# Rows of w, u and g turned by TensorE, an early activation table, and later DMA transposes in a fused linear-attention and MLP kernel

## The chip, the cores and the metric

The kernel runs on one core of a Trainium2 chip. The time is device microseconds (us) of one execution, taken as the median of several. Runs that lie over 1.5% above the fastest of the same kernel are called slow and left out of ratios. Five engines work side by side: TensorE (matmuls, "PE" in the profile, with its weight loads as "PEld"), VectorE (DVE), ScalarE (ACT), GpSimd (POOL) and SyncE (SP), which here mostly issues transfers for the DMA engines.

## The reference, cut to what matters

A linear-attention recurrence with a decay `w` per head and channel and a bonus `u` for the present token, then layer normalization and a two-layer MLP with a residual. There are 4 sequences of 768 tokens, 8 heads of 48 channels (384 in all) and 1536 hidden units.

```python
def _attn_ref(r, k, v, w, u):                      # (4, 8, 768, 48)
    state = np.zeros((B, H, D, D))
    for t in range(S):
        cur = np.einsum('bhd,bhe->bhde', u[None] * kt, vt)
        y[:, :, t] = np.einsum('bhd,bhde->bhe', rt, state + cur)
        state = w[None, :, :, None] * state + np.einsum('bhd,bhe->bhde', kt, vt)

def _moe_ref(x, g_ln, w_ch1, w_ch2):               # x: (4, 768, 384)
    xn = (x - mu) / np.sqrt(var + 1e-06) * g_ln
    return x + np.maximum(xn @ w_ch1, 0.0) @ w_ch2
```

## The kernel before

The tokens are cut into 24 tiles of 128, six to a sequence. In each tile, k and r are scaled by powers of w (tables `Fk` and `Fr`), which turns the recurrence inside a tile into matmuls: scores `at` = k·r, masked to `A`; the bonus from `q` = k·r elementwise; the state `Z`; and `y` from `A`, the state and v. The result is normalized (`xn`) and turned (`xT`) for the MLP: "up" matmuls into `hp`, ReLU into `hT`, "down" matmuls into `o`, and the store.

The scores and up matmuls of this kernel read k and xn with channels on the partitions, so both are transposed. Early tiles do it on TensorE, with a copy out of PSUM by ScalarE or VectorE. Later tiles let a DMA do it, with no instruction on TensorE. The constants `KP` and `LNP` are the first tile that uses DMA for k and for xn.

```python
    def transposes_k(i):                      # tiles below KP: TensorE, then evacuate_k
        for q in range(HP):
            nc.tensor.transpose(out=tk_t[i][:, q, :], in_=sc[:, q, :], identity=ident[:])
    def transpose_k_by_dma(i):                # tiles from KP on
        kT_t[i] = trp.tile([P, HP, P], BF16, name="kT", bufs=NKT)
        nc.sync.dma_start_transpose(out=kT_t[i][:], in_=k_bufs[i % NSC].rearrange("p h d -> p (h d)"))
    ...                                       # ln_by_dma(i) does the same for xn, from tile LNP on
    group_len = [1] * 2 + [GT] + [1] * 2 + [GT] * ((NT - 6) // GT)
    LNP = 4
    KP = 8
```

The order of all instructions is made by a list scheduler when the kernel is built. It places one task after another on a planned clock, always the one that can start first. A task has an engine, a cost, needs and buffers. A transfer also has a share of the DMA engines' time (`load`) and an extra delay until it has landed (`lands`).

```python
                key = (pick[1] - (...), -pri)          # pick[1]: planned start; ties go to the higher pri
    ...
            if t["load"]:
                dma_at = max(dma_at, end) + t["load"]
                end = dma_at + t["lands"]
    ...
            add(f"kT{i}", "SP", 1.25, lambda i=i: transpose_k_by_dma(i), [f"sck{i}"], ..., load=0.67, lands=1.2)
            add(f"lc{i}", "SP", 1.2, lambda i=i: ln_by_dma(i), [f"xn{i}", f"xT{g}"], ..., load=0.5, lands=1.2)
```

Each engine is given its own list in that order. Where something in it is late, the traces show the engine idle: TensorE for 10.7 us in front of DMA transposes in the kernel before. TensorE's MLP matmuls are strewn between the steps of the recurrence to fill its time; what is left of them runs after the last tile. Until the MLP starts, TensorE also runs dummy matmuls on an identity (`o<-ident`, "warming"): 177 of them, busy for 14.5 us, in the kernel before.

At the start, w is read element by element into a column, and u, w and g in the same way by ScalarE's queue:

```python
    w_c = const.tile([P, CK], FP32, name="w_c")
    nc.sync.dma_start(out=w_c[:], in_=bass.AP(tensor=w.tensor, offset=w.offset, ap=[[1, P], [P, CK]]))
    ...
    for src, dst in ((w, w_p), (u, u_p)):
        for par in range(2):
            nc.scalar.dma_start(out=dst[par * DP : par * DP + D, :],
                in_=bass.AP(tensor=src.tensor, offset=src.offset + par * D, ap=[[1, D], [E2, HP]]))
    load(0, "v", nc.scalar)
    g_sb = const.tile([P, CK], FP32, name="g_sb")
    nc.scalar.dma_start(out=g_sb[:], in_=moe_g_ln.rearrange("(kc p) -> p kc", p=P))
```

In the profile these small loads take long for their size: the 1.5 KB of `w_c` land after 2.7 us and those of `g_sb` after 5.4, where the median load of v by SyncE, 192 KB, takes 4.2.

## Time and profile before

The time before is 171.41 us (171.04 to 171.57, three runs). The profiled execution spans 168.1 us from the first instruction to the last.

| before | us | share of the span |
|---|---|---|
| TensorE busy | 148.4 | 88% |
| VectorE busy | 108.9 | 65% |
| ScalarE busy | 96.8 | 58% |
| GpSimd busy | 88.2 | 52% |
| TensorE waiting for a DMA transpose | 10.7 | 6% |

The busiest engine is TensorE, so the question is what it does in the 19.7 us in which it is idle. The prediction below shows those lines of the profile and reads them. One mark of progress is used throughout: the start of a tile's last recurrence matmul, "y of tile n". In the kernel before, y of tile 4 starts at 34.22 us and y of tile 23, the last, at 128.81.

### The profile page before, as it was taken

The page shows a single profiled execution, that of the slowest core. Times are in us where ns is not written, and L with a number is a line of the kernel's source. Part 1 is how long each engine was busy: PE and PEld are TensorE (multiplying, and loading weights), DVE is VectorE, ACT ScalarE, POOL GpSimd, SP SyncE. Part 2 cuts the span into 40 slices and gives each one's busy share as a digit, 9 for nine tenths or more (in the row PEclk, how much of TensorE's full clock was granted, in tenths as well). Part 3 has the DMA queues.
Part 4 walks back from the last instruction along what each step waited for, and adds up shares of the span by engine and source line. Part 5 has one row for each costly group of instructions (what it writes and reads, how often), then busy time and mean ns, then how long its engine had stood idle before and what let it go on. Part 6 is the DMA issues. An engine that isn't in the chain of part 4 may idle for free.

```text
span 168.1 us, 4543 instructions
## 1 busy us (share of the span) xinstructions
PE 148.4 (88%) x1774; PEld 114.6 (68%) x1774; DVE 108.9 (65%) x226; ACT 96.8 (58%) x217; POOL 88.2 (52%) x133
## 2 busy tenths in 40 slices
PE   6988998999594999979399999879999999999991
PEld 6887887687473677656257776657867777777660
DVE  5689979977982799787667887578985111111141
ACT  0665787698582468655715686547776654553200
POOL 2299849667665489665544669947985100000000
PEclk9999999999998799999959999999999999999999
DMA  3998999989989999899997999989913131111122
GB/s 71 212 232 217 397 201 340 304 196 216 201 191 157 184 169 231 193 161 199 150 192 182 183 185 252 185 154 204 193 31 98 47 94 51 47 47 47 51 94 94
DMA packets 87316, 27.95 MB, mean 166 GB/s; under 512 B 81536, under 2 KB 86144, under 8 KB 87296
## 3 DMA queue, kind: packets, MB, share of 16 engines
q1 hardware_dynamic: 75552, 24.13, 70.5%
q10 hardware_dynamic: 11744, 3.54, 10.9%
q8 instruction: 14, 0.23, 0.6%
q14 instruction: 6, 0.05, 0.1%
HBM read 18.88 MB, written 4.72 MB: 140 GB/s over the span
## 4 chain that ended last, share of the span: by engine, by line
PE 49%; DMA 22%; POOL 9%; SPq 5%; DVE 4%; issue 4%; ACT 4%; POOLq 0%; DVEq 0%; ACTq 0%
PE hp L577 18%; PE o L603 16%; DMA kT<-sc 13%; DMA xT<-xn 6%; PE o L285 3%; DMA v<-in_v_dram 3%; SPq L188 3%; PE at L401 3%; POOL Vb L437 3%; SPq L182 3%; PE hp L603 2%; POOL rs L530 1%; POOL sc L351 1%; PE tr L381 1%; POOL w_sb L332 1%
## 5 line engine op out<-in xcount | busy, mean ns | idle before, releaser
L577 PE MATMUL hp<-xT,w_sb 128*128 128x256 bf16 (+1 forms) x504 | 59.2, 261 | 4.2 <-DMA xT<-xn 4.2
L588 ACT ACTIVATE hT<-hp 128x512 bf16<-128x512 f32 x72 | 42.5, 597 | 29.9 <-PE hp L577 28.9
L603 PE MATMUL o<-w_sb,hT 128*128 128x384 bf16 x264 | 54.2, 332 | 0.6 <-DVE ot L613 0.3
L577 PEld LDWEIGHTS <-w_sb 128*128 128x128 bf16 x504 | 42.8, 99 | 13.3 <-issue 3.6
L603 PEld LDWEIGHTS <-hT 128*128 128x128 bf16 x288 | 27.2, 99 | 13.7 <-issue 1.8
L613 DVE SCALAR_TENSOR_TENSOR ot<-o,rs,x 128x384 f32<-128x384 f32 x22 | 13.5, 615 | 28.9 <-PE o L603 28.6
L412 DVE TENSOR_TENSOR A<-at,mask 128x512 bf16<-128x512 f32 x48 | 30.9, 681 | 1.0 <-PE at L401 1.0
L437 POOL TENSOR_TENSOR Vb<-v,cc 128x384 f32<-128x384 f32 x24 | 20.4, 850 | 9.3 <-ACT cc L433 9.2
L351 POOL TENSOR_TENSOR sc<-r,Fr 128x384 bf16<-128x384 f32 x15 | 15.9, 1063 | 13.1 <-DMA r<-in_r_dram 5.9
L501 DVE SCALAR_TENSOR_TENSOR x<-y,Vb 128x384 f32<-128x384 f32 x24 | 13.2, 548 | 7.5 <-PE y L488 5.7
L514 ACT ACTIVATE xn<-x,sum 128x384 bf16<-128x384 f32 x24 | 14.7, 613 | 5.5 <-DVE x L501 5.3
L348 POOL TENSOR_TENSOR sc<-k,Fk 128x384 bf16<-128x384 f32 x15 | 16.0, 1064 | 1.8 <-DMA k<-in_k_dram 1.0
L394 DVE TENSOR_TENSOR q<-rT,kT 128x512 bf16<-128x512 bf16 x20 | 13.0, 648 | 5.2 <-DMA kT<-sc 4.9
L401 PE MATMUL at<-rT,kT 48*128 48x128 bf16 x192 | 10.0, 226 | 6.7 <-DMA kT<-sc 6.5
L285 PE MATMUL o<-ident 128*128 128x128 bf16 x177 | 14.5, 239 | 1.6 <-DVE ident L240 1.6
L387 ACT COPY rT<-tr 128x512 bf16<-128x512 bf16 x17 | 11.9, 739 | 5.3 <-PE tr L381 3.6
L530 POOL TENSOR_TENSOR rs<-rs,expo 128x1 f32<-128x1 f32 x24 | 13.5, 564 | 2.0
L521 ACT ACTIVATE sq<-x,sum 128x384 bf16<-128x384 f32 x24 | 14.5, 604 | 0.0
L464 DVE TENSOR_TENSOR Z<-s,WLZ 128x384 bf16<-128x384 f32 x20 | 11.0, 550 | 4.1 <-ACT cc L433 3.6
L285 PEld LDWEIGHTS <-ident 128*128 128x128 bf16 x177 | 12.3, 109 | 1.8 <-DVE ident L240 1.6
L401 PEld LDWEIGHTS <-kT 48*128 48x128 bf16 x192 | 5.6, 97 | 10.9 <-DMA kT<-sc 8.6
L433 ACT COPY cc<-s 128x8 f32<-128x8 f32 x24 | 4.0, 167 | 11.4 <-PE s L453 9.0
(72 smaller groups left out, 168.5 us busy)
## 6 DMA issues: line engine op xcount, KB each, us to landing
wst<-in_moe_w_ch_dram SPq DMA_DIRECT2D x6, 768.0 KB, 6.7
r<-in_r_dram SPq DMA_DIRECT2D x11, 384.0 KB, 5.1
k<-in_k_dram SPq DMA_DIRECT2D x22, 192.0 KB, 4.8
v<-in_v_dram SPq DMA_DIRECT2D x18, 192.0 KB, 4.2
out_dram<-ot SPq DMA_DIRECT2D x16, 192.0 KB, 2.4
out_dram<-ot ACTq DMA_DIRECT2D x8, 192.0 KB, 1.9
v<-in_v_dram ACTq DMA_DIRECT2D x6, 192.0 KB, 4.5
k<-in_k_dram ACTq DMA_DIRECT2D x2, 192.0 KB, 4.1
```

The lines of the kernel that those rows point to most:

```text
L285: nc.tensor.matmul(out=warm[:, :P], lhsT=ident[:], rhs=ident[:], start=True, stop=True)
L348: eng.tensor_tensor(out=k_bufs[i % NSC][:, :, :D], in0=k_t[i][:], in1=Fk[:], op=ALU.mult)
L351: eng.tensor_tensor(out=r_bufs[e % NSR][:, j, :, :D], in0=r_t[e][:, :, j * D : (j + 1) * D], in1=Fr[:, j], op=ALU.mult)
L401: nc.tensor.matmul(out=at_t[i][:, par, p, :], lhsT=kT_t[i][p0 : p0 + D, p, :], rhs=rT_t[i][p0 : p0 + D, p, :], start=True, stop=True,)
L412: nc.vector.tensor_tensor(out=A_t[i][:, par], in0=at_t[i][:, par], in1=mask[:].unsqueeze(1).to_broadcast([P, HP, P]), op=ALU.mult,)
L437: nc.gpsimd.tensor_tensor(out=Vb_t[i][:], in0=vf_t[i][:], in1=cc_t[i][:].unsqueeze(2).to_broadcast([P, H, D]), op=ALU.mult)
L514: nc.scalar.activation(out=xn_t[i][:], in_=x_t[i][:], func=ACT.Identity, bias=sum_t[i][:], scale=-float(C))
L521: nc.scalar.activation(out=sq[:], in_=x_t[i][:], func=ACT.Square, bias=sum_t[i][:], scale=-float(C), accum_out=sq_t[i][:])
L530: nc.gpsimd.tensor_tensor(out=rs_t[i][:], in0=rs_t[i][:], in1=expo[:], op=ALU.pow)
L577: nc.tensor.matmul(out=hp[:, f * gw : (f + 1) * gw], lhsT=w1_sb[:, n, kc, fb * P : (fb + 1) * P], rhs=xT_t[g][:, kc, :gw], start=(kc == 0) ...
L588: nc.scalar.activation(out=hT_t[g][:, nf * m : nf * (m + 1), :gw], in_=hp_t[g, m][:].rearrange("p (f t) -> p f t", f=nf), func=ACT.Relu,)
L603: nc.tensor.matmul(out=o_t[i][:, :C], lhsT=hT_t[g][:, fk, j * P : (j + 1) * P], rhs=w2_sb[:, fk, :], start=(fk == 0), stop=(fk == FK - 1),)
```

## The change

It has two parts. The **start** loads w, u and g as rows, turns them with TensorE, and has ScalarE make a small copy first, meant to bring its activation table load forward (it starts at 4.13 us in the profile before and at 0.72 after; late_table below takes the copy out again). The **plan** moves DMA transposes to later tiles (k from tile 14 instead of 8, xn from tile 8 instead of 4), plans each with 3.0 instead of 1.2 us of landing time, makes the first six MLP groups single tiles, and asks for w1 two loads earlier.

```diff
-                dma_at = max(dma_at, end) + t["load"]
+                dma_at = max(dma_at, end + 1.2) + t["load"]
...
-    w_c = const.tile([P, CK], FP32, name="w_c")
-    nc.sync.dma_start(out=w_c[:], in_=bass.AP(tensor=w.tensor, offset=w.offset, ap=[[1, P], [P, CK]]))
+    w_row = const.tile([CK, P], FP32, name="w_row")
+    nc.sync.dma_start(out=w_row[:], in_=w.rearrange("h d -> (h d)").rearrange("(kc p) -> kc p", p=P))
...
-            nc.scalar.dma_start(                 # four column loads of w and u, one of g: gone
+    first = const.tile([P, 1], FP32, name="first")
+    nc.scalar.copy(out=first[:], in_=expo[:])
     load(0, "v", nc.scalar)
...
+    nc.gpsimd.dma_start(out=rows[0:CK, :], in_=moe_g_ln.rearrange("(kc p) -> kc p", p=P))
+    for n, src in enumerate((w, u)):
+        nc.gpsimd.dma_start(out=rows[CK + n * HP : CK + (n + 1) * HP, :]...[:, :, :D], in_=src...)
...
+    nc.tensor.transpose(out=wps[:, :CK], in_=w_row[:], identity=ident_f[:CK, :CK])
+    w_c = const.tile([P, CK], FP32, name="w_c")
+    nc.vector.tensor_copy(out=w_c[:], in_=wps[:, :CK])
...
-    group_len = [1] * 2 + [GT] + [1] * 2 + [GT] * ((NT - 6) // GT)
+    group_len = [1] * 6 + [GT] * ((NT - 6) // GT)
-    LNP = 4
-    KP = 8
+    LNP = 8
+    KP = 14
...
-    N1, N2 = 10, 13
+    N1, N2 = 8, 13
...
-                load=0.67, lands=1.2)            # k by DMA
+                load=0.67, lands=3.0)
-            add(f"lc{i}", ... load=0.5, lands=1.2)    # xn by DMA
+            add(f"lc{i}", ... load=0.5, lands=3.0)
```

Cut here: smaller constants of the plan, the turning of the rows of g, w and u into `vec` in the middle of the first tile, and `Fk` copied by ScalarE.

More of the change, by code (lines that the diff above doesn't have):

```diff
@@ L30, in add @@
     def add(self, name, eng, cost, fn, needs=(), takes=(), gives=(), pri=0, load=0.0, kind=None,
-            alt=None, lands=2.4):
+            alt=None, lands=1.9):
         t = dict(name=name, eng=eng, cost=cost, fn=fn, needs=list(needs), takes=list(takes),
@@ L53, in order @@
         eng_at = {e: 0.0 for e in self.LAG}
-        eng_at["SP"], dma_at = 4.0, 5.0
+        eng_at["SP"], dma_at = 3.5, 5.9
         last_kind = None
@@ L188, in load @@
         eng.dma_start(out=dst[:], in_=src[b, :, s0 : s0 + L, :].rearrange("h t d -> t h d"))
-    w_c = const.tile([P, CK], FP32, name="w_c")
-    nc.sync.dma_start(out=w_c[:], in_=bass.AP(tensor=w.tensor, offset=w.offset, ap=[[1, P], [P, CK]]))
+    w_row = const.tile([CK, P], FP32, name="w_row")
+    nc.sync.dma_start(out=w_row[:], in_=w.rearrange("h d -> (h d)").rearrange("(kc p) -> kc p", p=P))
     load(0, "r", nc.sync)
     load(0, "k", nc.sync)
-    w_p = const.tile([P, HP], FP32, name="w_p")
-    u_p = const.tile([P, HP], FP32, name="u_p")
-    nc.vector.memset(w_p[:], 0.0)
-    nc.vector.memset(u_p[:], 0.0)
-    for src, dst in ((w, w_p), (u, u_p)):
-        for par in range(2):
-            nc.scalar.dma_start(
-                out=dst[par * DP : par * DP + D, :],
-                in_=bass.AP(tensor=src.tensor, offset=src.offset + par * D, ap=[[1, D], [E2, HP]]),
-            )
+    NR = CK + 2 * HP
+    rows = const.tile([NR, P], FP32, name="rows")
+    nc.vector.memset(rows[:], 0.0)
+    expo = const.tile([P, 1], FP32, name="expo")
+    nc.vector.memset(expo[:], -0.5)
+    first = const.tile([P, 1], FP32, name="first")
+    nc.scalar.copy(out=first[:], in_=expo[:])
     load(0, "v", nc.scalar)
-    g_sb = const.tile([P, CK], FP32, name="g_sb")
-    nc.scalar.dma_start(out=g_sb[:], in_=moe_g_ln.rearrange("(kc p) -> p kc", p=P))
     NW = 3
@@ L240 @@
     nc.vector.tensor_copy(ident[:], ident_f[:])
-    expo = const.tile([P, 1], FP32, name="expo")
-    nc.vector.memset(expo[:], -0.5)
+    nc.gpsimd.dma_start(out=rows[0:CK, :], in_=moe_g_ln.rearrange("(kc p) -> kc p", p=P))
+    for n, src in enumerate((w, u)):
+        nc.gpsimd.dma_start(
+            out=rows[CK + n * HP : CK + (n + 1) * HP, :].rearrange("q (e d) -> q e d", e=2)[:, :, :D],
+            in_=src.rearrange("(q e) d -> q e d", e=2),
+        )
     expl = const.tile([P, 1], FP32, name="expl")
@@ L254, with keep_warm @@
     nc.vector.memset(uwI[:], 0.0)
+    warm = ps.tile([P, 512], FP32, name="o")
+    def keep_warm(n):
+        for _ in range(n):
+            nc.tensor.matmul(out=warm[:, :P], lhsT=ident[:], rhs=ident[:], start=True, stop=True)
     T = const.tile([P, CK, 2 * L], FP32, name="T")
@@ L272, in powers @@
         )
+    keep_warm(12)
+    wps = ps.tile([P, 512], FP32, name="s")
+    nc.tensor.transpose(out=wps[:, :CK], in_=w_row[:], identity=ident_f[:CK, :CK])
+    w_c = const.tile([P, CK], FP32, name="w_c")
+    nc.vector.tensor_copy(out=w_c[:], in_=wps[:, :CK])
     for kc in range(CK):
@@ L279 @@
         powers(T2[:, kc], w_r, kc)
-    warm = ps.tile([P, 512], FP32, name="o")
-    def keep_warm(n):
-        for _ in range(n):
-            nc.tensor.matmul(out=warm[:, :P], lhsT=ident[:], rhs=ident[:], start=True, stop=True)
-    keep_warm(38)
+    keep_warm(10)
     Fr = const.tile([P, 2, H, D], FP32, name="Fr")
@@ L297, with turn_rows, copy_rows, bonus_weights @@
         src = fps[:, :C].rearrange("p (h d) -> p h d", h=H)
-        if j < 2:
-            nc.scalar.copy(out=Fr[:, j], in_=src)
-        else:
-            nc.vector.tensor_copy(out=Fk[:], in_=src)
+        nc.scalar.copy(out=Fr[:, j] if j < 2 else Fk[:], in_=src)
+    vec = const.tile([P, NR], FP32, name="vec")
+    vps = ps.tile([P, 512], FP32, name="s")
+    w_p, u_p = vec[:, CK : CK + HP], vec[:, CK + HP : NR]
     g_neg = const.tile([P, CK], FP32, name="g_neg")
     wl = const.tile([P, HP], FP32, name="wl")
+    def turn_rows():
+        nc.tensor.transpose(out=vps[:, :NR], in_=rows[:], identity=ident_f[:NR, :NR])
+    def copy_rows():
+        nc.vector.tensor_copy(out=vec[:], in_=vps[:, :NR])
     def negate_g():
-        nc.vector.tensor_scalar(out=g_neg[:], in0=g_sb[:], scalar1=-1.0 / C, scalar2=None, op0=ALU.mult)
-    def bonus_weights():
+        nc.vector.tensor_scalar(out=g_neg[:], in0=vec[:, :CK], scalar1=-1.0 / C, scalar2=None, op0=ALU.mult)
+    def bonus_weights(eng):
         for par in range(2):
             p0 = par * DP
-            nc.gpsimd.tensor_tensor(
+            eng.tensor_tensor(
                 out=uwI[p0 : p0 + D, :, par], in0=u_p[p0 : p0 + D, :], in1=w_p[p0 : p0 + D, :], op=ALU.mult
@@ L316, in chunk_decay @@
     def chunk_decay():
-        nc.gpsimd.tensor_tensor(out=wl[:], in0=w_p[:], in1=expl[:].to_broadcast([P, HP]), op=ALU.pow)
+        nc.gpsimd.tensor_tensor(out=wl[:], in0=w_p, in1=expl[:].to_broadcast([P, HP]), op=ALU.pow)
     def spread_decay():
@@ L632 @@
     NU = {g: FK * n * P // 512 for g, n in enumerate(group_len)}
-    add("Fr", "ACT", 6.5, None, pri=99)
-    add("Fk", "DVE", 6.8, None, pri=99)
-    for name, lands in (("r0", 5.2), ("k0", 6.3), ("v0", 7.3), ("g", 8.5)):
+    add("scan", "DVE", 5.65, None, pri=99)
+    add("Fr", "ACT", 5.9, None, pri=99)
+    add("Fk", "ACT", 0.65, None, needs=["Fr"], pri=99)
+    for name, lands in (("r0", 5.4), ("k0", 6.4), ("v0", 7.5), ("rows", 5.5)):
         add(name, "", lands, None, pri=99, takes={"r0": [("r", 0, 2)], "k0": [("k", 0, 1)], "v0": [("vf", 0, 2)]}.get(name, []))
-    add("uw", "POOL", 0.45, bonus_weights, needs=["scr00"], pri=70)
-    add("wl", "POOL", 1.05, chunk_decay, needs=["uw"], pri=70)
+    add("turn", "PE", 0.15, turn_rows, needs=["rows", "Fk", "TR0", "TK0"], pri=70, takes=[("s", "vec", 1)])
+    add("vec", "DVE", 0.15, copy_rows, needs=["turn"], pri=70, gives=[("s", "vec")])
+    add("uw", "DVE", 0.3, bonus_weights, needs=["scr00", "vec"], pri=70, alt=[("POOL", 0.5)])
+    add("wl", "POOL", 1.1, chunk_decay, needs=["uw"], pri=70)
     add("WLZ", "ACT", 0.7, spread_decay, needs=["wl", "rT0", "kT0"], pri=70)
-    add("gn", "DVE", 0.2, negate_g, needs=["g", "A01"], pri=70)
+    add("gn", "DVE", 0.2, negate_g, needs=["vec", "A01"], pri=70)
     seq = [(a, i) for e in range(NT // 2) for a, i in (("r", 2 * e), ("k", 2 * e), ("v", 2 * e), ("k", 2 * e + 1), ("v", 2 * e + 1))]
-    N1, N2 = 10, 13
+    N1, N2 = 8, 13
     seq[N2:N2] = [("w2l", n) for n in range(NW)]
@@ L655 @@
         elif i and a == "r":
-            add(f"r{i // 2}", "SP", 0.6, lambda e, i=i: load(i, "r", e), takes=[("r", i // 2, 2)], pri=pri, load=1.58,
+            add(f"r{i // 2}", "SP", 0.6, lambda e, i=i: load(i, "r", e), takes=[("r", i // 2, 2)], pri=pri, load=1.5,
                 alt=[("ACT", 0.5)])
@@ L659 @@
             add(f"{a}{i}", "SP", 0.6, lambda e, i=i, a=a: load(i, a, e),
-                takes=[("k", i, 1)] if a == "k" else [("vf", i, 2)], pri=pri, load=1.05, alt=[("ACT", 0.5)])
+                takes=[("k", i, 1)] if a == "k" else [("vf", i, 2)], pri=pri, load=1.03, alt=[("ACT", 0.5)])
     for n in range(NW):
@@ L675 @@
         add(f"sckb{i}", "", 0.0, None, [], [("sck", i, 1 if last else 2)], pri=p0)
-        add(f"sck{i}", "DVE", 0.7, lambda e, i=i: scale_k(i, e), [f"k{i}", "Fk", f"sckb{i}"] + (["scr01"] if i == 0 else []), [], [("k", i)], pri=p0,
+        add(f"sck{i}", "DVE", 0.7, lambda e, i=i: scale_k(i, e), [f"k{i}", "Fk", f"sckb{i}"], [], [("k", i)], pri=p0,
             alt=[("POOL", 1.0)])
@@ L684 @@
                 [("scr", e)], pri=p0)
-        add(f"rT{i}", "ACT", 0.74, lambda g, i=i: evacuate_r(i, g), [f"TR{e}"], [("rT", i, 1)], [("tr", ("r", e))], pri=p0,
+        add(f"rT{i}", "ACT", 0.74, lambda g, i=i: evacuate_r(i, g), [f"TR{e}"] + (["kT0"] if i == 1 else []), [("rT", i, 1)], [("tr", ("r", e))], pri=p0,
             alt=[("DVE", 0.74)])
@@ L728 @@
         else:
-            add(f"lc{i}", "SP", 1.2, lambda i=i: ln_by_dma(i), [f"xn{i}", f"xT{g}"], [], [("xn", i)], pri=90, load=0.5, lands=1.2)
+            add(f"lc{i}", "SP", 1.2, lambda i=i: ln_by_dma(i), [f"xn{i}", f"xT{g}"], [], [("xn", i)], pri=90, load=0.5, lands=3.0)
         for m in range(NM):
@@ L745 @@
             add(f"re{g}_{m}", "ACT", 0.6, lambda g=g, m=m: relu(g, m), [f"up{g}_{m}"], [], [("hp", (g, m))], pri=30)
-    pe_at = 6.9
+    pe_at = 6.1
     for t in plan.order():
```

## The prediction

> **What bounds the kernel now.** I read the shares of the engines first, then the windows, then the waits of TensorE, then the first microseconds of the timeline, then the landing of the DMA transposes.
>
> The page, busy time of each engine, and two rows of its slices:
>
> ```profile
> PE 148.4 (88%) x1774; PEld 114.6 (68%) x1774; DVE 108.9 (65%) x226; ACT 96.8 (58%) x217; POOL 88.2 (52%) x133
> ...
> PEclk9999999999998799999959999999999999999999
> DMA  3998999989989999899997999989913131111122
> ```
>
> TensorE is busy 148.4 of 168.1 us, no other engine for over 65%. It is not busy for 19.7 us: 1.6 before its first matmul, 3.7 after its last (the last output tile and its store), so some 14.4 in between. The clock row has two dips, and the DMA row is full until about 122 us, then empty.
>
> Four windows (busy time and instructions of PE, PEld, DVE, ACT, POOL; granted clock; DMA share; GB/s):
>
> ```profile
> 50.00:55.00 5.00, 2.54 (x31) 1.78 (x30) 1.69 (x4) 1.69 (x5) 3.25 (x6) 0.87 0.91 150
> 55.00:60.00 5.00, 5.00 (x71) 3.64 (x70) 3.88 (x9) 2.89 (x7) 2.37 (x4) 0.79 1.00 206
> 80.00:85.00 5.00, 2.04 (x30) 1.45 (x28) 3.01 (x7) 2.80 (x7) 2.87 (x5) 0.94 1.29 164
> 85.00:90.00 5.00, 5.00 (x48) 3.46 (x47) 2.86 (x6) 1.32 (x4) 1.67 (x4) 0.72 0.95 156
> ```
>
> TensorE loses half a window twice, and each time the next window runs at a lower clock (0.79, 0.72). After 130 us it is solid: 15.00 of 15.00 us in 135 to 150.
>
> Who TensorE waited for (total us, times, longest):
>
> ```profile
> PE at L401 <- DMA kT<-sc: 6.5, 6, 3.0
> PE hp L577 <- DMA xT<-xn: 4.2, 2, 2.5
> PE o L285 <- DVE ident L240: 1.6, 1, 1.6
> PE tr L381 <- DVE sc L351: 0.9, 1, 0.9
> ```
>
> Of the 14.4 us inside, 10.7 (6.5 + 4.2) are waits for transposes made by DMA: of k (kT) for the scores, and of the normalized rows (xT) for the up matmuls. [...] This is the target.
>
> The start, from the timeline:
>
> ```profile
> 3.52 1.05 DVE L265 TENSOR_TENSOR_SCAN T<-w_c,ones 128x127 f32<-128x127 f32 x3 [0.81 <-DMA w_c<-in_w_dram]
> 4.13 1.28 ACT L276 ACT_TABLE_LOAD   x1 [4.13 <-DVE T L265]
> 5.42 0.70 ACT L276 COPY T<-T 128x128 f32<-128x128 f32 x3
> 6.60 0.86 ACT L299 COPY Fr<-hp 128x384 f32<-128x384 f32 x2 [0.48 <-PE hp L296]
> 7.54 1.00 POOL L351 TENSOR_TENSOR sc<-r,Fr 128x384 bf16<-128x384 f32 x1 [5.73 <-ACT Fr L299]
> ```
>
> The powers of w end at 4.57, yet their copies begin at 5.42, behind the table load; everything on r waits for Fr.
>
> The transposes, seen by tile kT (issue, then landing):
>
> ```profile
> L374 SPq DMA_TRANSPOSE kT<-sc x16: 1188/1217/1511, 50.8 to 121.8; - x16
> ...
> DMA to landing us min/median/max: 2.4/4.1/6.2
> ```
>
> xT reads 2.3/3.7/5.9. The kernel's list scheduler plans kT at 1.25 + 0.67 + 1.2 = 3.1 us: below the median, half the maximum.
>
> [...] 1.5 KB of g took 5.4 us to land and w_c 2.7, while 192 KB of v took 4.2. [...]
>
> **The change part by part.** Times for TensorE work are from the chain: six up matmuls of 256 columns 0.65 us, twelve of 128 columns 0.66, four down matmuls 0.65, a transpose 0.056, a warming matmul 0.057. Counts are from the order of instructions as built for both kernels.
>
> 1. *Transposes back on TensorE.* DMA transposes fall from 36 to 26 (kT 16 to 10, from tile 14 on; xT 20 to 16, from tile 8 on). TensorE gets 24 + 12 transposes: 36 x 0.056 = +2.0 us. Tiles 2 and 3 are no longer a pair: 72 more up matmuls of 128 columns (72 x 0.055 = 4.0) for 36 fewer of 256 (36 x 0.109 = 3.9): +0.1. Fixed TensorE work goes from 127.0 to 129.1 us. ScalarE makes most of the added copies out of PSUM: 6 of kT at 0.58 and 4 of xT at 0.48, +5.4 us, and takes Fk. VectorE loses Fk and gives six k scalings to GpSimd, and takes three of r back.
>
> 2. *Waits.* Both xT waits (1.70 before 43.98, 2.46 before 53.02) are of tiles 4 and 5, which now use TensorE: gone. The kT waits fall on tiles 11 to 19; those of 11 to 13 (0.38, 1.00 and 0.15) lose their DMA, the other 5.0 us are now planned with 1.25 + 1.2 + 0.67 + 3.0 = 6.1 us, about the maximum seen. I leave 1.5 us of the 10.7. [...] window by window, 0.13, 0.21, 0.06 and 0.28 of 5 us are 3.4 us, of which some 2.9 fell on work.
>
> 3. *Start.* [...] I take the scan to begin where it did (3.5). The table load is out of the path, so the copies follow the scan: Fr about 1.0 us earlier. The first loads (r0 lands about 6) and the weights limit how much survives: I keep 0.7 us at tile 4. Warming matmuls fall from 177 to 154 (-1.3 us), which shows the same gain and isn't added.
>
> 4. *The sum*, by the last matmuls of the recurrence (y) per tile. Before, y of tile 4 began at 34.22 and of tile 23 at 128.81: 94.6 us for 77.2 us of TensorE work that stands between them. The loss of 17.4 is 10.7 of DMA waits, 2.9 of clock and 3.8 of small things. In tiles without a wait the pace equals the TensorE work (tile 17: 3.52 us for 3.5 us). In the new order 74.7 us stand between the same two, as more MLP is left for the end (38.5 us after the last y, was 35.3). So: y of tile 4 at 33.5; + 74.7 + 3.8 + 1.5 left of DMA waits + 1.5 because the other engines are fuller = 115.0; + 38.5 + 3.9 (y itself, last output, store) = 157.4 us of span. Against 168.1 that is -10.7, so the time goes from 171.4 to about 160.7; I say 160.5.
>
> **The rivals.** *The other engines become the bound.* VectorE did 95.9 us of work in 10 to 130 us (80%). With about 91 us in the 105 us of the new plan it is near 87%, ScalarE and GpSimd about 83%. For it: the ring is tighter, 11 to 13 us of TensorE work between the release of a k buffer and the scores four tiles on, in tiles 16 to 21, was 14 to 16. Against it: VectorE held 86% from 90 to 105 us with TensorE 98% busy. It would end the recurrence at 119 or so: 165.
>
> *The DMA engines are the bound.* About 23.9 MB moved in 2 to 122 us at 199 GB/s. If that rate were the ceiling, ten transposes fewer (about 1.2 MB by tile size) save 6 us: y of tile 23 at 123, time 168. For it: the full DMA row. Against it: loads hold VectorE and GpSimd only 5.2 us from 50 to 125 us, other windows reach 231 to 245 GB/s[...].
>
> *The wait moves to the early tiles.* Weights w1 are now asked for before k and v of tile 3, and rows come through the GpSimd queue. If they are late for the first bonus (11.5 us), or tile 3 starves, a wait of 1 to 3 us appears before tile 4: 162 to 164.
>
> *All goes well*: no transpose wait left and fuller engines cost nothing: 157.5.
>
> **Range and chances.** Full mechanism gives 157.5, the central sum 160.5, one rival in part 163 to 166, the DMA ceiling 168. 8 in 10: 156.5 to 166. Two per cent is 168.0: it takes the DMA ceiling or two rivals at once to miss that: faster 0.90, same 0.09, slower 0.01.
>
> **What would show it.** TensorE waits for kT and xT together under 3 us; no clock slice under 9 after the first ten; y of tile 23 near 115 us and then about 38 us of solid MLP; Fr done near 6.5 instead of 7.46; TensorE busy about 146 to 149 us in a span near 157. It is wrong if the recurrence ends after 119: then the releasers of TensorE's waits name the rival (VectorE, GpSimd, ScalarE, or loads of k, v, r). A late vec row, or waits for ScalarE's copies in the place of DMA, would show that the latency was only moved.

## The result, and the profile after

The kernel after takes 165.83 us (median of four runs, 164.30 to 166.86, the last a slow run); the kernel before took 171.22 us in the same rounds. A ratio here is the mean time of one kernel's fast runs over that of the other's of the same rounds, so it is not quite the ratio of the medians: 0.966, with a 95% interval of 0.957 to 0.976. The change is faster by 5.4 us. The prediction was 10.9 us faster, at 160.5; its range of 156.5 to 166.0 holds the result just inside its upper end.

The page of the kernel after, the lines that answer to those of before (busy us, share and instructions; granted clock and DMA share in 40 slices):

```profile
PE 148.3 (91%) x1825; PEld 116.2 (71%) x1825; DVE 104.0 (64%) x221; ACT 103.0 (63%) x231; POOL 92.9 (57%) x139
...
PEclk9999999999999999999998799999999999999999
DMA  4999999997997999889999898785203221111122
```

The span is 163.3 us, 4.8 shorter, at the same 148.3 us of TensorE work. One of the two clock dips is gone, the other is still there. The DMA row is still full for its first two thirds.

TensorE's waits after (total, times, longest):

```profile
PE at L412 <- DMA kT<-sc: 4.0, 2, 2.5
PE o L261 <- DVE ident L236: 1.6, 1, 1.6
PE s L433 <- POOL q L405: 1.6, 1, 1.6
PE o L614 <- POOL w_sb L353: 1.0, 1, 1.0
```

No wait for xT is left. The waits for kT fell from six to two, but those two are long: 2.45 us in tile 16 and 1.56 in tile 21. A wait of 1.6 us for GpSimd's `q` is new; GpSimd came to it late, having stood idle for 1.14 us until 102.46 for a load of k. New too is one of 1.0 us for a copy of w2 (`w_sb`), at 28 us.

Windows after (busy time and instructions of PE, PEld, DVE, ACT, POOL; granted clock; DMA share; GB/s):

```profile
40.00:45.00 5.00, 3.61 (x57) 2.77 (x57) 4.20 (x8) 3.01 (x8) 4.05 (x5) 1.00 1.08 247
50.00:55.00 5.00, 4.99 (x62) 4.04 (x59) 3.88 (x9) 4.18 (x10) 3.35 (x7) 1.00 0.88 194
85.00:90.00 5.00, 2.55 (x32) 1.77 (x30) 2.26 (x4) 2.44 (x6) 3.31 (x5) 0.88 0.86 143
90.00:95.00 5.00, 5.00 (x59) 3.81 (x58) 4.38 (x12) 3.24 (x9) 3.26 (x7) 0.77 0.86 169
```

The window from 50 to 55 us, where the kernel before lost half to a late xT, is full. The one from 85 to 90 us is half empty, and the clock of the next is 0.77, which together cost tile 16 4.0 us (2.45 of waiting and, estimated from the clock readings of the two windows, some 1.5 of slower work).

The window from 40 to 45 us was not among those the prediction looked at. This is the same window of the kernel before:

```profile
40.00:45.00 5.00, 3.30 (x49) 2.47 (x46) 4.16 (x8) 3.39 (x8) 3.22 (x4) 1.00 1.03 231
```

Before, TensorE lost 1.70 us here, and the profile named one wait for xT, of exactly that length. After, the xT wait is gone, yet TensorE still loses 1.39: three short waits for VectorE (0.33 + 0.36 + 0.71), with loads behind them. The chain of work that ended last runs in this stretch through SyncE's issues and then through the load of r that was issued at 37.48 and landed at 42.27. Removing the wait that was named bought 0.3 us here.

How the transpose of tile 16 came to be late is seen in SyncE's timeline (start, us, what):

```profile
79.57 0.57 SPq L188 DMA_DIRECT2D k<-in_k_dram  x1
80.20 0.57 SPq L182 DMA_DIRECT2D r<-in_r_dram  x1
80.87 0.74 SPq L188 DMA_DIRECT2D v<-in_v_dram  x1
81.72 1.93 SPq L385 DMA_TRANSPOSE kT<-sc  x1
```

and in TensorE's:

```profile
89.18 0.61 PE L412 MATMUL at<-rT,kT 48*128 48x128 bf16 x8 [2.45 <-DMA kT<-sc]
```

GpSimd had scaled k at 79.41, the transpose was issued at 81.72 behind loads of k, r and v on the same queue, and it landed at 89.13. That is 7.4 us, the slowest of all:

```profile
L385 SPq DMA_TRANSPOSE kT<-sc x10: 1194/1213/2378, 71.3 to 110.7; - x10
...
DMA to landing us min/median/max: 2.4/4.2/7.4
```

The landing times of kT were 2.4/4.1/6.2 before. There are fewer transposes, and the single one has not become faster.

The start, from the timelines of the engines:

```profile
0.72 1.28 ACT L201 ACT_TABLE_LOAD   x1 [0.72 <-PEq L784]
...
3.50 1.05 DVE L272 TENSOR_TENSOR_SCAN T<-w_c,ones 128x127 f32<-128x127 f32 x3
...
3.95 0.92 ACT L288 COPY T<-T 128x128 f32<-128x128 f32 x3 [1.75 <-DVE T L272]
...
6.66 0.99 POOL L362 TENSOR_TENSOR sc<-r,Fr 128x384 bf16<-128x384 f32 x1 [2.93 <-ACT Fr L303]
```

TensorE reads the row of w at 3.00 us, where the column of before kept the scan waiting until 3.52; with the transpose and the copy to `w_c` (3.30, 0.16 us) the scan begins at 3.50 all the same. The copies begin at 3.95 instead of 5.42, and Fr is done at 6.57 instead of 7.46. Of that 0.9 us, y of tile 4 keeps 0.44 in this trace: 33.78 instead of 34.22. Five of the runs below (early_tr, short_lat, kt_pe, all_pe, late_tr) have the same instructions in the same order up to 36 us, and in them y of tile 4 comes at 32.96, 32.85, 33.06, 32.97 and 34.12. So one trace fixes this gain no better than to a range from 0.1 to 1.4 us.

### The profile page after: what moved, and what is told of

Read it like the earlier page. It is cut to its first block, busy times and chain, and to the rows that moved or that the text cites. A ratio compares the mean times of both kernels' runs of the same rounds, so it can differ in the third digit from the quotient of the medians.

```text
span 163.3 us, 4644 instructions
## 1 busy us (share of the span) xinstructions
PE 148.3 (91%) x1825; PEld 116.2 (71%) x1825; DVE 104.0 (64%) x221; ACT 103.0 (63%) x231; POOL 92.9 (57%) x139
## 4 chain that ended last, share of the span: by engine, by line
PE 41%; SPq 22%; DMA 19%; POOL 9%; issue 5%; DVE 2%; ACT 1%; POOLq 0%; DVEq 0%; ACTq 0%
PE o L614 17%; PE hp L588 15%; SPq L188 14%; DMA kT<-sc 7%; DMA r<-in_r_dram 6%; SPq L182 5%; DMA v<-in_v_dram 3%; POOL sc L359 3%; POOL Vb L448 3%; DMA k<-in_k_dram 3%; PE hp L614 2%; PE at L412 2%; POOL sc L362 1%; SPq L210 1%; PE tr L392 1%
## 5 line engine op out<-in xcount | busy, mean ns | idle before, releaser
L588 PE MATMUL hp<-xT,w_sb 128*128 128x256 bf16 (+1 forms) x540 | 58.1, 251 | 0.4 <-POOL w_sb L343 0.2
L614 PE MATMUL o<-w_sb,hT 128*128 128x384 bf16 x264 | 53.1, 329 | 1.0 <-POOL w_sb L353 1.0
L588 PEld LDWEIGHTS <-w_sb 128*128 128x128 bf16 x540 | 43.6, 98 | 8.2 <-POOL w_sb L343 0.7
L624 DVE SCALAR_TENSOR_TENSOR ot<-o,rs,x 128x384 f32<-128x384 f32 x22 | 13.5, 614 | 33.7 <-PE o L614 33.5
L359 POOL TENSOR_TENSOR sc<-k,Fk 128x384 bf16<-128x384 f32 x21 | 22.0, 1049 | 3.8 <-DMA k<-in_k_dram 2.0
L405 DVE TENSOR_TENSOR q<-rT,kT 128x512 bf16<-128x512 bf16 x21 | 14.1, 673 | 4.5 <-DMA kT<-sc 3.7
L362 POOL TENSOR_TENSOR sc<-r,Fr 128x384 bf16<-128x384 f32 x12 | 13.3, 1109 | 6.2 <-ACT Fr L303 2.9
L398 ACT COPY rT<-tr 128x512 bf16<-128x512 bf16 x18 | 12.9, 736 | 2.8 <-PE tr L392 1.6
L261 PE MATMUL o<-ident 128*128 128x128 bf16 x154 | 12.4, 234 | 1.6 <-DVE ident L236 1.6
L475 DVE TENSOR_TENSOR Z<-s,WLZ 128x384 bf16<-128x384 f32 x20 | 10.9, 547 | 1.9 <-ACT cc L444 1.6
L261 PEld LDWEIGHTS <-ident 128*128 128x128 bf16 x154 | 10.2, 106 | 1.9 <-DVE ident L236 1.6
L368 ACT CAST vv<-v 128x384 bf16<-128x384 f32 x10 | 5.1, 513 | 6.9 <-DMA v<-in_v_dram 6.9
```

What stands on the lines that cost most here:

```text
L261: nc.tensor.matmul(out=warm[:, :P], lhsT=ident[:], rhs=ident[:], start=True, stop=True)
L359: eng.tensor_tensor(out=k_bufs[i % NSC][:, :, :D], in0=k_t[i][:], in1=Fk[:], op=ALU.mult)
L362: eng.tensor_tensor(out=r_bufs[e % NSR][:, j, :, :D], in0=r_t[e][:, :, j * D : (j + 1) * D], in1=Fr[:, j], op=ALU.mult)
L588: nc.tensor.matmul(out=hp[:, f * gw : (f + 1) * gw], lhsT=w1_sb[:, n, kc, fb * P : (fb + 1) * P], rhs=xT_t[g][:, kc, :gw], start=(kc == 0) ...
L614: nc.tensor.matmul(out=o_t[i][:, :C], lhsT=hT_t[g][:, fk, j * P : (j + 1) * P], rhs=w2_sb[:, fk, :], start=(fk == 0), stop=(fk == FK - 1),)
```

## The experiments

Twelve kernels were run, in three calls; each ran beside the kernel before on its own chip, whose medians were 171.42, 170.52 and 170.44 us. "Work" below is TensorE's work without the warming matmuls, counted from the order of instructions with the durations that the prediction lists; "lost" is the time from y of tile 4 to y of tile 23 less the work between them. Before it is 94.6 - 77.2 = 17.4 us, after 87.0 - 74.7 = 12.3.

### Which part of the change carries the gain

**start_only** has the new start and the plan of before (the constants of the second half of the diff undone: group_len, LNP 4, KP 8, N1 10, lands 1.2, and so on).

```diff
-    LNP = 8
-    KP = 14
+    LNP = 4
+    KP = 8
-                load=0.67, lands=3.0)
+                load=0.67, lands=1.2)
...
```

> The start of the changed kernel (rows of w, u and g turned by TensorE, early activation table) with the plan of the kernel before (DMA transposes from tiles 4 and 8 on, short planned latency). My theory: the recurrence starts about 1.5 us earlier at tile 0 and 0.5 us at tile 4, and everything after is as before, with its 10 us of TensorE waits for DMA transposes: ratio 0.993, between 0.985 and 1.000. Rival: the earlier start is the larger part of the gain of 5.4 us; then 0.975 or less.

Measured: 167.49 us (167.04 to 169.32), ratio 0.981 (0.974 to 0.989). That is more than the start was expected to give, yet the second half of y of tile 4 comes at 34.04 (the first at 33.44), so that y ends only 0.3 us earlier than before (34.31 against 34.58). Whether the gain reaches 2% is unclear. The waits for kT and xT are still 4.7 and 3.8 us, at other tiles than before. The scheduler had made another order from the shifted start, so the gain beyond some tenths can't be put down to the start itself.

**plan_only** has the old start and the new plan.

```diff
-    LNP = 4
-    KP = 8
+    LNP = 8
+    KP = 14
-                load=0.67, lands=1.2)
+                load=0.67, lands=3.0)
...
```

> The new plan on the old start. My theory: it carries nearly all of the gain: waits for DMA transposes fall from 10.7 to 3 to 5 us, ratio 0.970 to 0.975 (the changed kernel has 0.966). Rival, if the start carries it: 0.99 or more.

Measured: 166.54 us (166.15 to 168.99, the last a slow run), ratio 0.973 (0.967 to 0.979). One wait of 0.5 us for kT is left, less than the 3 to 5 expected; instead there are many small ones for ScalarE, VectorE and GpSimd (the longest 2.2 us, for hT). The plan alone gives 2.7% and the start alone 1.9%, which add up to more than the 3.4% of both; but the three intervals together leave room of some 1.3%, so it is not shown whether the parts are independent.

### The two halves of the plan

**early_tr** is the kernel after with the transposes back at the early tiles, but the long planned landing kept.

```diff
-    LNP = 8
-    KP = 14
+    LNP = 4
+    KP = 8
```

> The changed kernel with the DMA transposes again from tiles 4 (rows) and 8 (k) on, still planned with the long latency of 3.0. Theory A (the planned latency was what mattered): waits for DMA transposes stay under 5 us, ratio 0.965 to 0.975. Theory B (taking the transposes off the DMA queue while the loads fill it is what mattered[...]): the waits before 60 us come back, 3 us or more, ratio 0.98 to 0.99.

Measured: 166.73 us (165.12 to 168.28), ratio 0.972 (0.964 to 0.979). The profiled run was a slow one, so its waits are only a hint: 3.4 us for kT in six waits of at most 1.0, and a dozen small ones for VectorE, ScalarE and GpSimd. The ratio is where theory A put it: with the transposes back at the early tiles, most of the gain stayed.

**short_lat** is the opposite: the later transposes, planned as short as before.

```diff
-                load=0.67, lands=3.0)
+                load=0.67, lands=1.2)
...                                   # the same for xn
```

> The changed kernel with the planned landing of the transposes put back from 3.0 to 1.2, transposes still from tiles 8 and 14 on. Theory A (latency mattered): waits for DMA transposes of 6 us or more after 65 us, ratio 0.98 to 0.99. Theory B (moving mattered): ratio 0.965 to 0.975, no slower than the changed kernel.

Measured: 164.00 us (163.49 to 164.57), ratio 0.960 (0.953 to 0.966). Undoing the long planned landing does not slow the kernel; it is no worse than the whole change. So the prediction's reason, that 6.1 us of planned time covers the slowest landing seen, is not needed for the gain. Nor, by early_tr, is the later place: either half of the plan without the other keeps most of it, and the runs do not rank the two. The waits of short_lat:

```profile
PE at L412 <- DMA kT<-sc: 1.8, 1, 1.8
PE o L261 <- DVE ident L236: 1.6, 1, 1.6
PE hp L588 <- DMA xT<-xn: 0.9, 1, 0.9
```

The first of them, and a window just after it:

```profile
91.66 0.61 PE L412 MATMUL at<-rT,kT 48*128 48x128 bf16 x8 [1.81 <-DMA kT<-sc]
...
92.00:94.00 2.00, 2.00 (x17) 1.01 (x13) 2.00 (x6) 1.67 (x4) 2.00 (x4) 0.50 0.43 92
```

The clock is at half for the whole window, with TensorE fully busy, after an idle time of 1.81 us. In plan_only a longer gap was followed by no dip (the clock reads 1.00 from 90 to 110 us):

```profile
101.60 0.81 PE L577 MATMUL hp<-xT,w_sb 128*128 128x256 bf16 x6 [2.17 <-ACT hT L588]
```

The clock reads 0.50 from 53.69 to 57.10 us and from 84.41 to 87.82 in the kernel before, and from 88.84 to 92.25 in the kernel after: 3.41 us each time. 0.77 or 0.88 are means over a window that holds part of such a stretch. Work in it took longer: in the kernel after, the eight score matmuls at 89.18 took 0.61 us (0.40 at 83.36), and the four down matmuls at 89.72 took 1.46 (0.81 at 84.89). What sets off such a stretch is not shown. Idle times of 2.46 and 2.96 us came with the two of the kernel before and one of 2.45 with that of the kernel after; the 1.70 us in the kernel before and the 2.17 in plan_only came with none.

### Taking the DMA transposes away

**kt_pe** turns k of all tiles on TensorE; xn still goes by DMA from tile 8.

```diff
-    KP = 14
+    KP = 24
```

> The changed kernel with every transpose of k on TensorE; only rows from tile 8 on go by DMA. It pays 40 transposes of 0.056 us (2.2 us of TensorE) and ten copies of 0.58 us, mostly on ScalarE. Theory A (the two late kT transposes of tiles 16 and 21 and the lowered clock behind the first are what is left over the prediction): 4.0 + 1.6 us gone for 2.2 us paid, so 3 us under the changed kernel: 161 to 163. Theory B (VectorE, ScalarE and GpSimd, or the loads, hold the recurrence anyway): the waits for kT turn into waits for the other engines, 165 to 168.

Measured: 164.85 us (164.64 to 166.82), ratio 0.972 (0.964 to 0.980). The wait for kT is gone, but the time is above the 161 to 163 us of theory A. TensorE's largest wait in the profiled run (the longest of the four) is now one for VectorE:

```profile
PE y L499 <- DVE A L423: 4.2, 2, 3.9
```

VectorE's timeline shows what held it just before, when it should have gone on to the mask `A` of that tile (TensorE's matmul followed at 85.71):

```profile
84.69 0.36 DVE L368 CAST vv<-v 128x384 bf16<-128x384 f32 x1 [5.18 <-DMA v<-in_v_dram]
```

The two waits for kT, 4.0 us together, were replaced by one of 3.9, and behind it stands a load of v that was 5.18 us late for VectorE. Without DMA transposes of k the loads themselves are what is late.

**all_pe** uses no DMA transpose at all.

```diff
-    LNP = 8
-    KP = 14
+    LNP = 24
+    KP = 24
```

> No DMA transpose at all: 40 + 48 more transposes on TensorE (4.9 us), 10 copies of 0.58 and 16 of 0.48 us more on ScalarE (13.5 us on 103). Theory A: no wait for a DMA transpose, clock full throughout, about the same time as the changed kernel (5.6 us gone, 4.9 paid): 163 to 166. Theory B (ScalarE becomes the bound): TensorE waits for ScalarE's copies, 167 to 171.

Measured: 164.20 us (164.06 to 164.65), ratio 0.966 (0.961 to 0.971). TensorE is busy for 151.6 us, 3.3 more than after, and idle for 10.8 instead of 15.0. No wait is over 1.6 us. The most steady of the kernels, and no slower than the change. But it still loses 2.9 of the 20 us from 30 to 50 us, as the kernel after loses 2.1: in these 20 us neither has a DMA transpose in flight.

### Letting transposes go ahead of loads

**yield2** has the scheduler hold each plain load back by 2 us, so that transposes and stores get in front of them in SyncE's queue.

```diff
+                plain = t["load"] and t["first"][0] == "SP" and t["name"][:2] not in ("kT", "lc", "st")
-                key = (pick[1] - (...), -pri)
+                key = (pick[1] + (2.0 if plain else 0.0) - (...), -pri)
```

> The changed kernel, with the scheduler told to let a load of k, v or r wait up to 2 us for other work that is about to be ready, so that a DMA transpose gets into the SP queue ahead of loads rather than behind them. Theory A (transposes are late because they stand behind loads in the queue): the longest landing falls from 7.4 to 5 us or less and waits for kT fall from 4.0 to under 2: 161 to 164. Rival: loads that start later starve the recurrence instead: 166 to 170, with waits for DMA of r, k and v on GpSimd and VectorE.

This one computed a wrong result (relative error 0.058), which was not intended. Its order shows why: the scheduler counts k buffers as nameless slots, while the kernel picks buffer i mod 4. With the held loads, the scaling of k of tile 14 was placed ahead of the last reader of tile 10, which uses the same buffer. The check for races before the run doesn't see this, as the program then waits correctly for what it was told. The time (166.29, ratio 0.979) is therefore not used, and whether the idea works is left open.

### Fewer loads, with the order of instructions kept

The next two are wrong on purpose. Only v of tiles 0 and 1 is loaded; all later tiles read these two again. That takes 22 loads of 192 KB away, 4.3 MB of 26.8 or 28.0, and nothing else but their issues: the instructions of TensorE, VectorE and GpSimd are the same ones in the same order, in both kernels.

```diff
     def load(i, what, eng):
+        if what == "v" and i >= 2:
+            vf_t[i] = vf_t[i % 2]
+            return
```

**no_v** does this to the kernel after.

> Wrong result on purpose: v is loaded for tiles 0 and 1 only and used again for the others, so 22 of 192 KB loads are gone (4.3 of 18.9 MB read), and the order of instructions on TensorE, VectorE and GpSimd is the same. Theory A (the DMA queue is what makes transposes late and holds the first 42 us, where the chain of waits runs through SP's issues of loads): the wait for kT goes below 1 us, and tile 4's last matmul comes 2 us earlier or more: 157 to 160. Theory B (the order and the other engines hold it): within 1.5 us of the changed kernel, 164 to 166.

Measured: 154.01 us (153.93 to 157.69, the last a slow run), ratio 0.906 (0.899 to 0.913). These are all of TensorE's waits that the profile lists:

```profile
PE o L264 <- DVE ident L239: 1.6, 1, 1.6
PE s L436 <- POOL q L408: 0.7, 1, 0.7
PE s L436 <- DVE q L408: 0.2, 1, 0.2
```

No wait for kT is left, at the same planned places. The window from 40 to 45 us is full:

```profile
40.00:45.00 5.00, 5.00 (x86) 4.21 (x83) 4.99 (x11) 3.62 (x11) 3.93 (x6) 1.00 0.38 87
```

and the median landing of kT fell from 4.2 to 2.8 us:

```profile
DMA to landing us min/median/max: 2.4/2.8/5.4
```

Lost is 77.9 - 74.7 = 3.2 us instead of 12.3. This is the clearest result of the study: with the same work in the same order, these loads account for some 9 us of the 12.3, through late transposes and through late data. Another 2 us come before it, as y of tile 4 starts at 31.81. It is more than the expectation of 157 to 160.

**before_no_v** does the same to the kernel before.

> Wrong result on purpose: the kernel before, v loaded for tiles 0 and 1 only. Its planned landing of a DMA transpose is still the short one. Theory A (loads in the DMA queue made the transposes late): waits for DMA transposes fall from 10.7 to under 3 us and the time to 155 to 160, though the plan is the old one. Theory B (the plan was too short whatever the traffic): waits of 5 us or more remain, 162 or more.

Measured: 156.27 us (155.86 to 158.27, the last a slow run), ratio 0.914 (0.907 to 0.921). The profile is of the slow run, so I read only its kinds of waits. The landings of kT are 2.4/2.8/5.8, and one wait of 2.3 us remains for the scores of tile 14, where the kernel before had its longest for kT. The profile names a square on ScalarE as its releaser, but TensorE's weight load for the same scores, and VectorE's `q` of that tile, name the transpose:

```profile
73.91 0.23 PEld L404 LDWEIGHTS <-kT 48*128 48x128 bf16 x8 [2.37 <-DMA kT<-sc]
73.92 0.40 PE L404 MATMUL at<-rT,kT 48*128 48x128 bf16 x8 [2.26 <-ACT sq L524]
```

This kT was issued at 68.02 and took 5.8 us. So one late transpose is left here, of 10.7 us of such waits before.

So with fewer loads the two kernels differ by 2.3 us instead of 5.4 (medians of two calls, whose kernels before agree within 0.1 us). The intervals of the two ratios overlap, so the 2.3 is rough; but more than half of the change's gain seems to be there only while all the loads are: it is gained from lateness that the loads bring.

### Transposes after the loads

**late_tr** follows from this: keep DMA transposes only where few loads are left.

```diff
-    LNP = 8
-    KP = 14
+    LNP = 18
+    KP = 20
```

> The changed kernel with DMA transposes only at the very end: k from tile 20, rows from tile 18, when most loads have landed. TensorE pays 24 + 30 transposes (3.0 us), ScalarE mostly 6 copies of 0.58 and 10 of 0.48 us (8.3 us). Theory A (a transpose costs something only where it shares the DMA queue with loads): the waits for kT (4.0), the lowered clock (1.6) and some of the load waits go, 161 to 164, as good as or better than the kernel without any DMA transpose (164.2). Theory B (the fuller ScalarE and TensorE take it back): 164 to 167.

Measured: 162.87 us (161.88 to 164.97, the last a slow run), ratio 0.952 (0.942 to 0.962). The result is right. TensorE is busy for 150.5 of 161.3 us, the clock row of its page reads 9 in all 40 slices (mean granted clock 0.998), and the ten transposes left are not waited for. The top of its waits:

```profile
PE o L261 <- DVE ident L236: 1.6, 1, 1.6
PE s L433 <- DVE q L405: 1.4, 2, 1.2
PE tr L563 <- DVE kT L381: 1.2, 1, 1.2
```

It beats the kernel before clearly and has the lowest median of all kernels with a right result. Against the kernel after (0.966) it was not run in the same rounds, and the two intervals overlap by half a per cent, so a gain over it of some 1.5% is likely, not settled.

### How much is due to the order alone

**jitter** is the kernel after with the scheduler's priorities shifted at random, by up to 2 for each kind of task. Needs, costs, buffers and constants are the same.

```diff
-    for t in plan.order():
+    for t in plan.order(spread=2.0, seed=1):
```

> The changed kernel with the scheduler's ties broken by a random seed: same instructions, same planned costs, another order. No theory of the change predicts a difference; what it differs by is how far one order is from another at no intended change. I expect within 2 us of the changed kernel (164 to 168). If it is 2 us or more off, then differences of 1 to 2 us between the versions of the plan (short against long planned landing, transposes of k on TensorE) are of that size too and say nothing of their edit.

Measured: 171.47 us (170.70 to 171.91), ratio 1.003 (0.995 to 1.011). A single other order of the same tasks costs as much as the whole change gains. Here y of tile 1 comes at 23.26 instead of 15.01, and much of that is made up later. It is a harsh sample: the scheduler put in 218 warming matmuls (154 in the kernel after), so the late start was at least in part in its own plan already. One seed is one sample, but it warns of what may be read from experiments that reorder: differences of 1 or 2 us between start_only, plan_only, early_tr, short_lat and kt_pe can't be put down to their edit. The two runs without v, which keep the order, can be read without this doubt.

### The table load

**late_table** takes the early copy out again, so that the table would be loaded at the first copy of T as before.

```diff
-    first = const.tile([P, 1], FP32, name="first")
-    nc.scalar.copy(out=first[:], in_=expo[:])
```

> The changed kernel without the early copy[...]: the load of 1.28 us comes back before the first copy of the powers, the order of everything else is the same. Theory A (TensorE's own queue and the loads set the pace after the start): Fr comes 0.8 to 1.3 us later, but tile 4 at most 0.5 us and the end 0 to 0.7 us: 165.5 to 166.5. Theory B (the start is worth what it saves): the end moves by 1 us or more, 167 and up.

Measured: 167.72 us (165.28 to 169.48; 168.06 and 169.48 count as slow), ratio 0.974 (0.961 to 0.987). The edit did not do what it was meant to. ScalarE's first microseconds:

```profile
0.72 0.43 ACTq L188 DMA_DIRECT2D v<-in_v_dram  x1
1.19 1.28 ACT L286 ACT_TABLE_LOAD   x1 [1.19 <-PEq L782]
```

The table load did not go back behind the scan; it follows the issue of v, which ended at 1.15, and is over at 2.47, while the first copy of T comes at 3.96. Fr was done at 6.22, no later than with the early copy. In the kernel before, ScalarE was issuing the columns of w, u and g until 4.09:

```profile
3.50 0.59 ACTq L206 DMA_DIRECT2D g_sb<-in_moe_g_ln_dram  x1
```

The table load came at 4.13 (in before_no_v, with the same start, at 4.12, after the same issue). In all three, the load starts 0.03 to 0.04 us after the issue before it on ScalarE has ended. Whether the column loads held it up is not shown: no run puts them back alone.

As the order of instructions is that of the kernel after, the run also serves as a repeat of it. It lies at 165.3 to 167.4 in its fast runs. In its profiled run, a slow one, kT waits are 5.0 us and tile 16 alone loses 5.1. Against the expectation it says nothing, as the load was not delayed.

### All runs side by side

TensorE's idle time is the span less its busy time, in the profiled run. yield2 is left out, as its result was wrong without intent.

| kernel | median us | ratio to before | TensorE busy | idle | waits named for kT + xT |
|---|---|---|---|---|---|
| before | 171.4 | 1 | 148.4 | 19.7 | 10.7 |
| after | 165.8 | 0.966 | 148.3 | 15.0 | 4.0 |
| start_only | 167.5 | 0.981 | 149.1 | 16.2 | 8.5 |
| plan_only | 166.5 | 0.973 | 148.4 | 16.4 | 0.5 |
| early_tr (slow profile) | 166.7 | 0.972 | 147.8 | 18.1 | 3.4 |
| short_lat | 164.0 | 0.960 | 148.9 | 13.0 | 2.7 |
| kt_pe | 164.9 | 0.972 | 152.5 | 12.5 | none |
| all_pe | 164.2 | 0.966 | 151.6 | 10.8 | none |
| late_tr | 162.9 | 0.952 | 150.5 | 10.8 | none |
| jitter | 171.5 | 1.003 | 154.5 | 15.5 | none |
| late_table (slow profile) | 167.7 | 0.974 | 150.2 | 17.5 | 5.8 |
| no_v (wrong on purpose) | 154.0 | 0.906 | 145.4 | 6.7 | none |
| before_no_v (wrong on purpose, slow profile) | 156.3 | 0.914 | 145.9 | 10.3 | 2.3 (see above) |

"None" means none among TensorE's largest waits. Read plan_only and jitter with care: hardly a transpose is late there, yet TensorE idles as much as in the kernel after. Removing this kind of wait is not enough.

## Why the prediction was right or wrong

The direction was right, and the mechanism in part: TensorE waited for DMA transposes, the change takes most of those waits away (10.7 us to 4.0), and the time falls by more than 2%. But taking a wait away did not always give its time back, as the loads stood behind it. The size was off by a factor of two; that the median lies inside the range is partly luck, as two of the four runs (166.57 and 166.86) lie above it. The sum of the prediction's step 4, term by term:

| term | predicted | measured |
|---|---|---|
| y of tile 4 starts | 33.5 | 33.8 |
| TensorE work to y of tile 23 | 74.7 | 74.7 |
| DMA waits left | 1.5 | 4.0 |
| lowered clock | 0 | 1.5 |
| small things and fuller engines | 3.8 + 1.5 | 6.8 |
| y of tile 23 starts | 115.0 | 120.8 |
| from there to the end | 42.4 | 42.5 |
| span | 157.4 | 163.3 |

Lowered clock, an estimate from the readings of two windows: 0.12 of the 2.55 us busy from 85 to 90, and 0.23 of the 5.00 from 90 to 95. The small things are what is left of the 12.3 us. Two readings in the prediction were off: it put 2.9 us of the lowered clock on work in the kernel before, but TensorE was busy through both dips (53.69 to 57.10 and 84.41 to 87.82), which makes it 3.4 and the small things 3.3; and the DMA engines moved 25.0 MB at 208 GB/s from 2 to 122 us, not 23.9 at 199.

**The start was right as far as it can be read.** Fr came at 6.57 ("near 6.5"), and 0.44 of the 0.7 us survived at tile 4 in this trace, 0.1 to 1.4 in the six with the same first 36 us. The mechanism given for the table load is in doubt: in late_table the load comes at 1.19 us without the early copy.

**The end and the counts were right.** After y of tile 23 come 42.5 us of solid MLP, and TensorE's busy time of 148.3 us lies in the range of 146 to 149.

**"Both xT waits ... gone" was right as a statement and wrong as a gain.** The wait at 53 us gave its time back. The one at 44 us did not: the window from 40 to 45 lost 1.70 before and 1.39 after. Loads were late in the same stretch, and only the last cause of a wait is named. no_v, in which that window is full, shows that the loads were behind it.

**"I leave 1.5 us of the 10.7" is the term that failed first.** It rested on planning 6.1 us for a transpose, "about the maximum seen". The maximum moved: 7.4 us after. And short_lat shows that the long plan wasn't needed for the gain. The landing time was not one figure that the plan could allow for: in no_v and before_no_v, with 22 loads fewer, the median falls from 4.2 and 4.1 to 2.8 us at the same plan.

**The sum held nothing for a lowered clock after the change, and that fell with it.** One gap of 2.45 us was left, and the clock read 0.50 for 3.41 us from 88.84 on, which cost an estimated 1.5 us of slower work beside the wait. The length of a gap alone did not tell when: in short_lat, 1.81 us of idling was followed by half the clock, and in plan_only 2.17 us was not.

**The rival "the DMA engines are the bound" was put aside too far.** Its number was wrong: y of tile 23 came at 120.8, not 123, and the time is 165.8, not 168. But its subject was right. I argued from averages, that loads held VectorE and GpSimd for only 5.2 us from 50 to 125 us and that other windows reached a higher rate. no_v measures it instead: taking 4.3 MB of loads away shortens the span by 11.2 us, 9.1 of them between y of tile 4 and of tile 23. What no run tells apart is by which way the loads delay a transpose: by the place in the queue, by sharing the DMA engines, or by SyncE's time to issue (a median of 1.21 us for a transpose of k in the kernel after, where the chain of work that ended last spends 22% of the span in SyncE's issues).

**The rival "the other engines become the bound" had a small part**: one wait of 1.6 us for GpSimd's q, and the one of 3.9 us for VectorE in kt_pe; behind the first stood a load of k, behind the second one of v. In no_v the same engines do the same work in 152.1 us, so they were no bound at 163.

**The rival "the wait moves to the early tiles"** came in part. Between y of tile 3 and of tile 4 TensorE idles for 1.8 us (0.4 in the kernel before), 1.0 of it for GpSimd's copy of w2, whose load was late; in no_v it idles for 0.1 there. And tile 6 loses 1.4, where the kernel before lost 1.7 to the wait for xT.

The misses together: 0.3 + 2.5 + 1.5 + 1.5 + 0.1 = 5.9 us of span. The time is only 5.3 us off, as the profiled run's time exceeded its span by 1.8 us (the prediction had taken 171.4 - 168.1 = 3.3), and the median lies 0.7 above the profiled run.

## What to carry to other kernels

A wait that the profile names shows only what came last. Before counting it as gain, ask of each such window what else was late in it, and test with a run that thins out that other thing and keeps the order, as leaving out v does here. DMA transposes issued among bulk loads here landed after a median of 4.2 us and up to 7.4, and after 2.8 with fewer loads, so try them where few loads are left, or on the matrix engine if that has the time; here both did at least as well as planning a longer latency (late_tr 162.9 us and all_pe 164.2, against 165.8). With a scheduler between the edit and the instructions, run a few random reorderings first: they show how large a difference must be before it means anything. And compare the traces of versions up to their first difference: that gives the scatter of one program for free.
